# A gMLP and S5 layer on one core: another start for the layer norms, another order of the output pairs with a column split in the last, and a held scaling of C

## The chip, the core and the metric

The kernel runs on one core of one Trainium2 chip. The metric is device microseconds of an execution; the 61 timed runs of the kernel before lie between 261.94 and 264.62 us (standard deviation 0.5). A gMLP is a gated MLP that also mixes rows; S5 is a linear recurrence over the rows. The engines are PE (TensorE, matmul), DVE (VectorE), ACT (ScalarE), POOL (GpSimd) and SP (SyncE, which here issues nearly all DMAs). The profile gives a *span* for each execution: from the core's first recorded instruction to its last. The *time* of the same execution is longer than the span (that difference written "time minus span" below).

## The reference, cut to what matters

```python
xn = layernorm(x)                        # x: 2048 x 640, bf16
# A: a diagonal complex recurrence over 2048 steps, 640 states
Bu = xn @ B_bar.T;  h[t] = Lam_bar * h[t-1] + Bu[t];  yA = 2 * real(h @ C.T) + xn * Dskip
# B: a gated MLP with a mix over rows
z  = gelu(xn @ w_in)                     # 640 -> 1728
z1, z2 = z[:, :864], layernorm(z[:, 864:])
yB = (z1 * (w_sp @ z2 + b_sp[:, None])) @ w_out
out = x + yA + yB
```

## The kernel before

The program is a list of operations with the memory that each reads and writes. A small list scheduler in the kernel's own source, with a guessed duration for each operation, fixes the order of DVE's, ACT's, POOL's and SP's instructions; PE keeps program order. So each change of an operation or a guess can reorder three engines for the whole run.

PE's order is: layer-norm rows transposed tile by tile (128 rows each) and multiplied by the second half of `w_in` (z2, whose results ACT passes through gelu), then `Bu`, then z1, then the row mix by Strassen-Winograd's seven products (the "spatial" stage), then eight output pairs, again by seven products each.

PE writes its results to the banks of a memory called PSUM; an *eviction* is the copy of such a result out of its bank, by ACT or DVE. The *pitch* is the usual distance from one matmul's start to the next.

The layer norm of tile `i`, and the transposition of its rows (cut). Tiles 0 to 5 are transposed by PE and copied from PSUM, tiles 6 to 15 by DMA:

```python
ACT_LN = (5, 8, 11)                  # statistics by two ACT passes; the others by DVE's bn_stats
DMA_T = tuple(range(6, 16))
def ln_x(i):
    if i in ACT_LN:
        act(... ACT.Copy, accum_out=stv[:, i, 0:1] ...)       # sum
        act(... ACT.Square, accum_out=stv[:, i, 1:2] ...)     # sum of squares
        dve(... mean = sum / D ...); dve(... mean * mean ...); dve(... var ...)
    else:
        dve(bn_stats); dve(bn_stats); dve(bn_aggr)
    dve(lambda e: e.tensor_scalar(stv[:, i, 14:15], stv[:, i, 13:14], 1e-5, None, op0=ALU.add), ...)
    pool(lambda e: e.tensor_tensor(rstd, stv[:, i, 14:15], C("half")[:, 0:1], ALU.pow), ...)
    dve(... xn = (x - mean) * rstd ...)
def xn_T(i):
    if i in DMA_T:
        dma("sp", xnTv[:, :, i * 128:(i + 1) * 128], xn.ap(D), ..., transpose=True); return
    pe(five transposes of 128 columns)
    if (i % 2 == 0 or i == 1) and i != 2: act(copy)           # ... else dve(copy)
```

The end of an output pair (cut). `X`, `V`, `W` are PSUM banks, `og` adds the last 96 rows of the sum, `store` is a DMA to the output:

```python
prod("P7", X, False)
# ACT copies X to W (in the last pair to two banks, 192 and 128 columns)
prod("P3", V, False); og(0, 1, V); add(c12); store(0)
prod("P4", X, False); og(1, 0, X); add(c21)
# last pair: store(c21 half, sp); for each part: og(1, 1, part); add(c22 part); store(part)
# other pairs: og(1, 1, W); add(c22); store(1)
```

Of the kernel before, what the change touches and what calls it, by code (L numbers as in the profile page):

```python
# [6 lines left out]
ALU = mybir.AluOpType  # L7
# [21 lines left out]
class _Graph:  # L29
# [57 lines left out]
    def schedule(self):  # L87
# [32 lines left out]
        while left:  # L120
# [23 lines left out]
            if op.nbytes:  # L144
                if op.lat > 2.2:
                    dma_free = max(st + 0.3, dma_free) + op.nbytes / self.DMA_BW_T
                    free[eng] = max(free[eng], dma_free)
                    op.done = max(st + op.occ, dma_free) + 1.7
                else:
                    at = max(st + op.occ + 0.9, dma_free)  # L150
                    dma_free = at + op.nbytes / (self.DMA_BW0 if at < self.DMA_T0 else self.DMA_BW)
                    op.done = dma_free + op.lat - 0.9
            else:
                op.done = st + op.occ + op.lat
# [50 lines left out]
D = 640  # L205
# [9 lines left out]
def bass_parallel_sum__ssm_conv_s5__mixer_gmlp__prompt_kernel(  # L215
# [17 lines left out]
    with _cl.ExitStack() as _stack, nc.Block() as block:  # L233
# [274 lines left out]

        ACT_LN = (5, 8, 11)
        EARLY = (0, 1, 2)  # L510
        HELD = ()
        XNB = 0.0
# [4 lines left out]
        LASTN = 480  # L517
        DMA_T = tuple(range(6, 16))
        xns = {}

        xc_m = z1o_m

        def ln_early(i):

            xm, xc = xs[i], xc_m[i]
            mean, rstd = mrv[:, i, 0:1], mrv[:, i, 1:2]
            mi, ri = mr_m.iv(i * 8, 4), mr_m.iv(i * 8 + 4, 4)
            if i < 2:
                act(lambda e: e.activation(xc.ap(D), xm.ap(D), ACT.Copy, scale=1.0 / D, accum_out=mean),
                    [xm.iv()], [xc.iv(0, 1280), mi], ca(D, acc=1), "lnmean%d" % i)  # L530
            else:
                mean, mi = stv[:, i, 12:13], siv(i, 12, 13)
                early_bn(i)
            dve(lambda e: e.tensor_scalar(xc.ap(D), xm.ap(D), mean, None, op0=ALU.subtract), [xm.iv(), mi], [xc.iv(0, 1280)],
                cd(D, 4) + PTR, "xc%d" % i)

        def early_bn(i):
            x, xm = xs[i].ap(D), xs[i]
            held = [xc_m[2].iv()] if i == 1 else []
            dve(lambda e: e.bn_stats(stv[:, i, 0:6], x[:, 0:320]), [xm.iv()] + held, [siv(i, 0, 6)], 0.41, "bn%da" % i)  # L540
# [4 lines left out]
        def ln_early_std(i):  # L545
            rstd, ri = mrv[:, i, 1:2], mr_m.iv(i * 8 + 4, 4)
            if i < 2:
                early_bn(i)
            dve(lambda e: e.tensor_scalar(stv[:, i, 14:15], stv[:, i, 13:14], 1e-5, None, op0=ALU.add),
                [siv(i, 13, 14)], [siv(i, 14, 15)], 0.07, "lne%d" % i)  # L550
            pool(lambda e: e.tensor_tensor(rstd, stv[:, i, 14:15], C("half")[:, 0:1], ALU.pow),
                 [siv(i, 14, 15), Civ("half")], [ri], 0.5, "rstd%d" % i)

        def ln_early_xn(i):
            xm, xn = xs[i], xn_m[i]
            xns[i] = xn
            mean, mi = (mrv[:, i, 0:1], mr_m.iv(i * 8, 4)) if i < 2 else (stv[:, i, 12:13], siv(i, 12, 13))
            dve(lambda e: e.tensor_scalar(xn.ap(D), xm.ap(D), mean, mrv[:, i, 1:2], op0=ALU.subtract, op1=ALU.mult),
# [4 lines left out]
        def ln_x(i):  # L563
# [4 lines left out]
            if i in ACT_LN:  # L568
                sq = xn_m[i]
                act(lambda e: e.activation(sq.ap(D), x, ACT.Copy, accum_out=stv[:, i, 0:1]),  # L570
                    [xm.iv()], [sq.iv(), siv(i, 0, 1)], ca(D, acc=1), "lnsum%d" % i)
                act(lambda e: e.activation(sq.ap(D), x, ACT.Square, accum_out=stv[:, i, 1:2]),
                    [xm.iv()], [sq.iv(), siv(i, 1, 2)], ca(D, acc=1), "lnsq%d" % i)
                dve(lambda e: e.tensor_scalar(mean, stv[:, i, 0:1], 1.0 / D, None, op0=ALU.mult),
                    [siv(i, 0, 1)], [mi], 0.07, "lnm%d" % i)
                dve(lambda e: e.tensor_tensor(stv[:, i, 2:3], mean, mean, ALU.mult),
                    [mi], [siv(i, 2, 3)], 0.07, "lnmm%d" % i)
                dve(lambda e: e.scalar_tensor_tensor(stv[:, i, 13:14], stv[:, i, 1:2], 1.0 / D, stv[:, i, 2:3],
                                                     op0=ALU.mult, op1=ALU.subtract),
                    [siv(i, 1, 3)], [siv(i, 13, 14)], 0.07, "lnv%d" % i)  # L580
            else:
# [5 lines left out]
                    "bna%d" % i)  # L587
            dve(lambda e: e.tensor_scalar(stv[:, i, 14:15], stv[:, i, 13:14], 1e-5, None, op0=ALU.add),
                [siv(i, 13, 14)], [siv(i, 14, 15)], 0.07, "lne%d" % i)
            pool(lambda e: e.tensor_tensor(rstd, stv[:, i, 14:15], C("half")[:, 0:1], ALU.pow),  # L590
                 [siv(i, 14, 15), Civ("half")], [ri], 0.5, "rstd%d" % i)
            xn = xn_m[i]
# [5 lines left out]
        def xn_T(i, b=None):  # L598
# [15 lines left out]
            if i == 0:  # L614
# [3 lines left out]
                    [xnT_m.iv(k * S * 2, 256) for k in (3, 4)], 0.21, "xnT0b")  # L618
            elif (i % 2 == 0 or i == 1) and i != 2:
                act(lambda e: e.copy(xnTv[:, :, i * 128:(i + 1) * 128], v), [bank(b)], xnT_iv(i, i + 1),  # L620
# [341 lines left out]

        def c_scaled():

            for q in range(5):
                for c, (src, nm) in enumerate(((A_C_re, "r"), (A_C_im, "i"))):
                    dma("sp", cpv[:, c, q, :].rearrange("p (o n) -> p o n", o=1), src[:, q * 128:(q + 1) * 128], [],
                        [cp_m.iv((c * 5 + q) * 1280, 1280)], D * 256, "C%s%d" % (nm, q), transpose=True)
            for q in range(5):
                k1, k2 = C("k")[:, q:q + 1], C("k")[:, 5 + q:6 + q]  # L970
# [3 lines left out]
                act(lambda e, o=ta, im=im, k2=k2: e.activation(o.ap(D), im, ACT.Identity, scale=k2),  # L974
                    [imi, Civ("k")], [ta.iv()], ca(D, ptr=1), "cy%d0" % q)
                act(lambda e, o=tb, re=re, k2=k2: e.activation(o.ap(D), re, ACT.Identity, scale=k2),
                    [rei, Civ("k")], [tb.iv()], ca(D, ptr=1), "cy%d1" % q)

# [55 lines left out]
        def ring(lst, n):  # L1034
            m = lst[n[0] % len(lst)]
            n[0] += 1
            return m

        def spatial(j, banks):
            X, Y, Z = banks  # L1040
# [52 lines left out]
            prod(X, "A22", "T4", False, "P4")  # L1093
            ev(half(c1, 0), X, b1, hiv(c1, 0), "c21_%d" % j)
            zm = z1i[j]
            for h, c in ((0, c0), (1, c1)):
# [85 lines left out]
        def out_pair(j, last=False):  # L1182
# [68 lines left out]
            prod("P7", X, False)  # L1251
            W = bk()
            if last:
                W2 = bk()
                parts = (("act", W, 0, 192), ("sp", W2, 192, HD))
            else:
                parts = (("sp", W, 0, HD),)
            for _, w, c0, c1 in parts:
                act(lambda e, w=w, c0=c0, c1=c1: e.copy(ps[:, w, c0:c1], ps[:, X, c0:c1]), [bank(X)], [bank(w)],  # L1259
                    ca(c1 - c0, psum=True), "u3%d_%d" % (c0, j))  # L1260
            prod("P3", V, False)
            og(0, 1, V)
            add(ov(0, 1), V, fv(t12), "c12b")
            store(0)
            prod("P4", X, False)
            og(1, 0, X)
            add(ov(1, 0), X, bv(1, 0), "c21b")
            def finish():
                for q, w, c0, c1 in parts:
                    og(1, 1, w, c0, c1)  # L1270
                    o = om[1].ap(HD, BF16, 640)
                    dve(lambda e, w=w, c0=c0, c1=c1, o=o: e.tensor_tensor(o[:, c0:c1], ps[:, w, c0:c1], f(t22)[:, c0:c1],
                                                                          ALU.add),
                        [bank(w), t22.iv(c0 * 4, (c1 - c0) * 4)], [om[1].iv(640 + c0 * 2, (c1 - c0) * 2)], cd(c1 - c0),
                        "c22b%d_%d" % (c0, j))
                    if last:
                        store(1, q, HD + c0, HD + c1)
                if not last:
                    store(1)
            if last:  # L1280
                store(1, "sp", 0, HD)
                finish()
            else:
                finish()

        EARLY_AT = (7, 8, 9)
        LATE = 3
        for i in EARLY:
            ln_early(i)
        for i in EARLY:  # L1290
            ln_early_std(i)
# [5 lines left out]
        for i in (3, 4):  # L1297
            ln_x(i)
        z2_mm(0, 0, 2, 2, 5)
# [68 lines left out]
        for gm in g_m:  # L1368
            pool(lambda e, gm=gm: e.memset(gm.ap(32, BF16, 1728), 0.0), [], [gm.iv(1728, 64)], 0.2, "gpad")
        c_scaled()  # L1370
        ct_comb()
        no = [0]
# [21 lines left out]
        for j in range(8):  # L1394
            load_z1(j)
            s_comb(j)
            spatial(j, (0, 1, 2) if j % 2 == 0 else (3, 4, 5))
            if j + 2 < 8:
                for a in ("A21", "A11", "A12", "A22"):
# [83 lines left out]
```

## Time and profile before

| | |
|---|---|
| time, median of the first 3 runs | 263.33 us (262.6 to 263.37) |
| span of the profiled execution (its time: 263.89 us) | 262.1 us |
| PE busy | 255.7 us (98%) |
| DVE busy | 244.6 us |

The waits view of the kernel before, for PE alone. Columns: engine, tile and line, what it waited for, microseconds in total, times, longest.

```profile
PE ps L649 <- DMA arena<-arena: 1.4, 1, 1.4
PE ps L490 <- DVE arena L477: 1.2, 1, 1.2
PE ps L670 <- ACT arena L620: 0.4, 1, 0.4
PE ps L611 <- DVE arena L534: 0.3, 1, 0.3
```

Nothing after 21 us is in this list: PE is dense from there to its last matmul but for three hiccups of 0.65 us together, and the starts of its matmuls lie 183 ns (432 columns) and 136 ns (320 columns) apart. So nearly all that can be shortened lies in the start and the end of the execution, for a change that takes no PE work away.

The timeline of the kernel before: PE around its longest wait, then the end on PE, DVE and ACT's queue. Columns: start, duration of the group, engine, line, operation, out<-in, shapes, count, and in brackets the idle time before it and what ended it.

```profile
13.66 0.44 PE L611 MATMUL ps<-arena 128*128 128x128 bf16 x5
13.94 1.08 PE L670 MATMUL ps<-arena 128*128 128x432 bf16 x5
14.89 0.90 PE L649 MATMUL ps<-arena 128*128 128x432 bf16 x4
...
17.21 2.00 PE L649 MATMUL ps<-arena 128*128 128x432 bf16 x10
20.62 0.72 PE L649 MATMUL ps<-arena 128*128 128x432 bf16 x3 [1.41 <-DMA arena<-arena]
...
258.71 0.44 PE L1213 MATMUL ps<-arena 96*128 96x320 bf16 x3
259.05 0.49 DVE L1227 TENSOR_TENSOR arena<-ps,arena 128x320 bf16<-128x320 f32 x1 [0.73 <-PE ps L1213]
259.46 0.55 DVE L1272 TENSOR_TENSOR arena<-ps,arena 128x192 bf16<-128x192 f32 x2
259.84 0.37 ACTq L373 DMA_DIRECT2D out_dram<-arena  x1
```

L611 are the transposes of a tile (five), L649 and L670 the z2 matmuls. At 20.62 PE has waited for tile 6's transpose by DMA; counted from matmul start to matmul start the stall is 1.58 us over the pitch. At the end three additions on DVE follow the last matmuls one after the other.

### The profile page before, as it was taken

Reading aid. Unit: us, or ns where it says so; the run is one execution under the profiler, and the core shown is the slowest. Engines: PE = TensorE matmul, PEld = TensorE weight load, DVE = VectorE, ACT = ScalarE, POOL = GpSimd, SP = SyncE. Lnnn points to the kernel's source line nnn. Section 1 sums busy time; section 2 is a strip of 40 time slices with the busy share of each in tenths; the row PEclk is TensorE's granted clock in tenths of the full one; section 3 lists DMA queues with packets and bytes.
Section 4 is the critical chain, followed back from the end, with each engine's and each line's share of the span. In section 5 each row is a group of like instructions: output and inputs, shape, how many; then the busy total and the mean of one; then the engine's idle time right before and its main releaser. Section 6 shows DMA issues by size and latency. Waiting matters only on the chain.

```text
span 262.1 us, 4316 instructions
## 1 busy us (share of the span) xinstructions
PE 255.7 (98%) x1488; PEld 151.4 (58%) x1488; DVE 244.6 (93%) x584; ACT 178.8 (68%) x322; POOL 22.6 (9%) x37
## 2 busy tenths in 40 slices
PE   7998999999999999999999999999999999999995
PEld 3544554444446777755555555555556777777773
DVE  5899999698999999999999999899999999999952
ACT  5698999989997445442333385795979996885110
POOL 2445155500000000000000000000000000000000
PEclk9999999999999999999999999999999999999999
DMA  6957859999405763298988968977533455645721
GB/s 196 347 94 123 190 116 238 260 310 188 47 0 117 189 184 135 103 315 141 196 171 180 224 142 200 170 195 188 146 103 105 138 118 133 164 134 151 185 92 54
DMA packets 90276, 42.48 MB, mean 162 GB/s; under 512 B 73006, under 2 KB 90254, under 8 KB 90254
## 3 DMA queue, kind: packets, MB, share of 16 engines
q1 hardware_dynamic: 90110, 42.16, 67.1%
q8 instruction: 12, 0.20, 0.3%
q14 instruction: 10, 0.08, 0.1%
q10 hardware_dynamic: 144, 0.05, 0.1%
HBM read 12.27 MB, written 12.45 MB: 94 GB/s over the span
## 4 chain that ended last, share of the span: by engine, by line
PE 65%; DVE 20%; DMA 8%; issue 4%; ACT 1%; POOL 0%; SPq 0%; DVEq 0%
PE ps L1206 23%; PE ps L649 18%; PE ps L743 16%; DVE arena L1016 5%; PE ps L1059 4%; DMA g_scratch<-arena 4%; DVE arena L794 2%; PE ps L670 2%; DMA arena<-arena 2%; PE ps L1213 2%; DVE arena L1132 1%; DMA arena<-in_B_w_sp_dram 1%; DVE arena L853 1%; DVE arena L1079 1%; DVE arena L772 1%
## 5 line engine op out<-in xcount | busy, mean ns | idle before, releaser
L1059 PE MATMUL ps<-arena 128*128 128x432 bf16 x448 | 82.1, 346 | 0.1
L1059 PEld LDWEIGHTS ps<-arena 128*128 128x128 bf16 x448 | 43.7, 98 | 38.3 <-ACT arena L1072 0.8
L1206 PE MATMUL ps<-arena 128*128 128x320 bf16 x448 | 64.6, 299 | 0.1
L1206 PEld LDWEIGHTS ps<-arena 128*128 128x128 bf16 x448 | 43.4, 98 | 18.1 <-ACT ps L1259 0.5
L649 PE MATMUL ps<-arena 128*128 128x432 bf16 x280 | 51.9, 346 | 1.4 <-DMA arena<-arena 1.4
L849 ACT ACTIVATE arena<-arena 128x512 bf16<-128x512 bf16 x70 | 46.2, 713 | 4.3 <-DVE arena L853 2.9
L649 PEld LDWEIGHTS ps<-arena 128*128 128x128 bf16 x280 | 34.5, 124 | 17.9 <-DMA arena<-arena 1.8
L743 PE MATMUL ps<-arena 128*128 128x512 bf16 x200 | 43.3, 379 | 0.0
L1072 ACT ACTIVATE arena<-ps,arena 128x432 f32<-128x432 f32 (+1 forms) x32 | 19.5, 618 | 22.4 <-PE ps L1059 19.3
L743 PEld LDWEIGHTS ps<-arena 128*128 128x128 bf16 x200 | 19.6, 98 | 23.5
L772 DVE SCALAR_TENSOR_TENSOR arena<-arena 128x512 f32<-128x512 bf16 x35 | 25.5, 742 | 0.1
L748 ACT CAST arena<-ps 128x512 bf16<-128x512 f32 x40 | 22.2, 610 | 3.0 <-PE ps L743 3.0
L1227 DVE TENSOR_TENSOR arena<-ps,arena 128x320 bf16<-128x320 f32 (+1 forms) x40 | 18.7, 483 | 5.8 <-PE ps L1213 4.4
L853 DVE TENSOR_TENSOR arena<-arena 128x1024 bf16<-128x1024 bf16 (+1 forms) x42 | 24.1, 592 | 0.0
L727 ACT ACTIVATE arena<-ps 128x864 bf16<-128x864 f32 x16 | 14.3, 891 | 13.9 <-PE ps L649 12.9
L1016 DVE TENSOR_TENSOR arena<-arena 128x1024 bf16<-128x1024 bf16 x32 | 21.2, 681 | 0.4 <-DMA arena<-in_B_w_sp_dram 0.4
L794 DVE TENSOR_TENSOR arena<-arena 128x512 f32<-128x512 f32 (+2 forms) x40 | 21.2, 547 | 0.0
L777 DVE SCALAR_TENSOR_TENSOR arena<-arena 128x256 bf16<-128x256 bf16 (+1 forms) x35 | 16.6, 476 | 0.0
L774 DVE SCALAR_TENSOR_TENSOR arena<-arena 128x256 bf16<-128x256 bf16 (+1 forms) x35 | 16.4, 474 | 0.0
L1235 ACT COPY ps<-ps 128x320 f32<-128x320 f32 x16 | 6.6, 414 | 13.9 <-PE ps L1206 13.9
L1173 DVE TENSOR_TENSOR arena<-arena 128x640 bf16<-128x640 bf16 x32 | 15.2, 480 | 0.0
L663 ACT ACTIVATE arena<-arena 128x864 bf16<-128x864 bf16 x12 | 11.2, 934 | 0.0
(117 smaller groups left out, 255.7 us busy)
## 6 DMA issues: line engine op xcount, KB each, us to landing
g_scratch<-arena SPq DMA_DIRECT2D x16, 224.0 KB, 2.9
z_scratch<-arena SPq DMA_DIRECT2D x16, 216.0 KB, 2.1
arena<-z_scratch SPq DMA_DIRECT2D x8, 432.0 KB, 4.2
arena<-in_A_x_dram SPq DMA_DIRECT2D x16, 160.0 KB, 3.6
base_scratch<-arena SPq DMA_DIRECT2D x16, 160.0 KB, 2.3
arena<-base_scratch SPq DMA_DIRECT2D x16, 160.0 KB, 2.7
out_dram<-arena SPq DMA_DIRECT2D x15, 160.0 KB, 2.1
arena<-in_B_w_in_dram SPq DMA_DIRECT2D x7, 216.0 KB, 4.0
```

What stands on the lines that cost most here:

```text
L649: r = e.matmul(ps[:, b + h, 0:FG], lhs(k), winv[:, k, hcol * FH + h * FG:hcol * FH + (h + 1) * FG], start=(k == 0), stop=(k == ND - 1))
L743: r = e.matmul(ps[:, b, :], btv[:, ri, k, q * 128:(q + 1) * 128], xnTv[:, k, tq * 512:(tq + 1) * 512], start=(k == 0), stop=(k == ND - 1))
L748: act(lambda e: e.copy(o[:, ri, tq], ps[:, b, :].rearrange("p (m j) -> p j m", j=8)), [bank(b)], [l_m.iv((q * 8 + j) * 1024 + ri * 512 + t ...
L772: dve(lambda e: e.scalar_tensor_tensor(tv, prev, lr, cur, op0=ALU.mult, op1=ALU.add), pr + [l_iv(q, j)] + cr, [t.iv()], cd(512) + PTR, nm ...
L794: tt = lambda o, a, b, op: (lambda e: e.tensor_tensor(o, a, b, op))
L849: act(lambda e, pv=pv, hv=hv, lo=lo, sc=sc: e.activation(pv, hv[:, lo:lo + 2, 1:257], ACT.Identity, scale=sc), [h.iv(), Civ(cn)], [m.iv((q ...
L853: dve(lambda e, mv=mv, lq=lq: e.tensor_tensor(lq, lq, mv, ALU.add), li + [m.iv(0, 1024 * n)], li, cd(512 * n, 2), "fix%s%d%d" % (nm, q0, j))
L1016: dve(lambda e: e.tensor_tensor(o.ap(1024), x.ap(1024), y.ap(1024), op), [x.iv(), y.iv()], [o.iv()], cd(1024, 2), "%s_%d" % (name, j))
L1059: r = e.matmul(ps[:, bk, 0:FG], lv_[:, k, :], rv[k], start=(first and k == 0), stop=(k == 7), skip_group_check=True)
L1072: act(lambda e: e.activation(o, pb(bk), ACT.Identity, bias=bias), [bank(bk)] + bi, [dst], ca(FG, psum=True, ptr=1), name)
L1206: r = e.matmul(ps[:, bk, c0:c1], lf(q), rf(q)[:, c0:c1], start=(first and q == 0), stop=(q == 7), skip_group_check=True)
L1227: dve(lambda e: e.tensor_tensor(o[0][:, c0:c1], ps[:, bk, c0:c1], y[0][:, c0:c1], ALU.add), [bank(bk), y[1]], [o[1]], cd(c1 - c0), "%s_%d" ...
```

## The change

Its intent: take tile 6 off the slow DMA transpose, relieve DVE in the start, let less work follow the last matmul, and keep C's scaling from running ahead of its load (the hold). The scheduler's guess for a DMA transpose is changed too. The diff, cut (marked `...`):

```diff
-                    dma_free = max(st + 0.3, dma_free) + op.nbytes / self.DMA_BW_T
-                    free[eng] = max(free[eng], dma_free)
-                    op.done = max(st + op.occ, dma_free) + 1.7
+                    dma_free = max(st + 1.25, dma_free) + op.nbytes / 270e3
+                    free[eng] = st + 0.65 + op.nbytes / 300e3
+                    op.done = dma_free + 2.2
...
-        ACT_LN = (5, 8, 11)
+        ACT_LN = (3, 6, 10)
+        ACTM = (0, 1)
+        LNE_DVE = (5, 6, 7)
...
-        DMA_T = tuple(range(6, 16))
+        DMA_T = tuple(range(7, 16))
...
-            dve(lambda e: e.tensor_scalar(stv[:, i, 14:15], stv[:, i, 13:14], 1e-5, None, op0=ALU.add),
+            (dve if i in LNE_DVE else pool)(
+                lambda e: e.tensor_scalar(stv[:, i, 14:15], stv[:, i, 13:14], 1e-5, None, op0=ALU.add),
...
-                dve(lambda e: e.tensor_scalar(mean, stv[:, i, 0:1], 1.0 / D, None, op0=ALU.mult), ...
-                dve(lambda e: e.tensor_tensor(stv[:, i, 2:3], mean, mean, ALU.mult), ...
...
-            elif (i % 2 == 0 or i == 1) and i != 2:
+            elif i in (1, 4, 6):
                 act(lambda e: e.copy(xnTv[:, :, i * 128:(i + 1) * 128], v), ...
...
-        c_scaled()
-        ct_comb()
+        c_load()
...
             spatial(j, (0, 1, 2) if j % 2 == 0 else (3, 4, 5))
+            if j == 3:
+                c_scale([u3_of[CY_AT]])        # held until spatial tile 3's u3
+                ct_comb()
...
+            og(1, 1, W)
+            add(ov(1, 1), W, fv(t22), "c22b")
+            if last:
+                store(1, "act", HD, D)
+            for n, (x, c0, c1) in enumerate(parts):     # last pair: 192 and 128 columns, two banks
+                prod("P4", x, False, c0, c1)
+                og(1, 0, x, c0, c1)
+                dve(... c21 columns c0:c1 ...)
+                if last:
+                    store(1, ("sp", "act")[n], c0, c1)
```

More of the change, by code (lines that the diff above doesn't have):

```diff
@@ L517, in bass_parallel_sum__ssm_conv_s5__mixer_gmlp__prompt_kernel @@
         LASTN = 480
-        DMA_T = tuple(range(6, 16))
+        DMA_T = tuple(range(7, 16))
         xns = {}
-        xc_m = z1o_m
+        xc_m = z1o_m + [xn_m[15]]
         def ln_early(i):
@@ L527, in ln_early @@
             mi, ri = mr_m.iv(i * 8, 4), mr_m.iv(i * 8 + 4, 4)
-            if i < 2:
+            if i in ACTM:
                 act(lambda e: e.activation(xc.ap(D), xm.ap(D), ACT.Copy, scale=1.0 / D, accum_out=mean),
@@ L538, in early_bn @@
             x, xm = xs[i].ap(D), xs[i]
-            held = [xc_m[2].iv()] if i == 1 else []
+            held = [xc_m[2].iv()] if i == 1 else xnT_iv(2, 3) if i == 3 else []
             dve(lambda e: e.bn_stats(stv[:, i, 0:6], x[:, 0:320]), [xm.iv()] + held, [siv(i, 0, 6)], 0.41, "bn%da" % i)
@@ L546, in ln_early_std @@
             rstd, ri = mrv[:, i, 1:2], mr_m.iv(i * 8 + 4, 4)
-            if i < 2:
+            if i in ACTM:
                 early_bn(i)
-            dve(lambda e: e.tensor_scalar(stv[:, i, 14:15], stv[:, i, 13:14], 1e-5, None, op0=ALU.add),
-                [siv(i, 13, 14)], [siv(i, 14, 15)], 0.07, "lne%d" % i)
+            (dve if i in LNE_DVE else pool)(
+                lambda e: e.tensor_scalar(stv[:, i, 14:15], stv[:, i, 13:14], 1e-5, None, op0=ALU.add),
+                [siv(i, 13, 14)], [siv(i, 14, 15)], 0.07 if i in LNE_DVE else 0.22, "lne%d" % i)
             pool(lambda e: e.tensor_tensor(rstd, stv[:, i, 14:15], C("half")[:, 0:1], ALU.pow),
-                 [siv(i, 14, 15), Civ("half")], [ri], 0.5, "rstd%d" % i)
+                 [siv(i, 14, 15), Civ("half")], [ri], 0.55, "rstd%d" % i)
         def ln_early_xn(i):
@@ L556, in ln_early_xn @@
             xns[i] = xn
-            mean, mi = (mrv[:, i, 0:1], mr_m.iv(i * 8, 4)) if i < 2 else (stv[:, i, 12:13], siv(i, 12, 13))
+            mean, mi = (mrv[:, i, 0:1], mr_m.iv(i * 8, 4)) if i in ACTM else (stv[:, i, 12:13], siv(i, 12, 13))
             dve(lambda e: e.tensor_scalar(xn.ap(D), xm.ap(D), mean, mrv[:, i, 1:2], op0=ALU.subtract, op1=ALU.mult),
@@ L569, in ln_x @@
                 sq = xn_m[i]
-                act(lambda e: e.activation(sq.ap(D), x, ACT.Copy, accum_out=stv[:, i, 0:1]),
-                    [xm.iv()], [sq.iv(), siv(i, 0, 1)], ca(D, acc=1), "lnsum%d" % i)
-                act(lambda e: e.activation(sq.ap(D), x, ACT.Square, accum_out=stv[:, i, 1:2]),
+                act(lambda e: e.activation(sq.ap(D), x, ACT.Copy, scale=1.0 / D, accum_out=mean),
+                    [xm.iv()], [sq.iv(), mi], ca(D, acc=1), "lnsum%d" % i)
+                act(lambda e: e.activation(sq.ap(D), x, ACT.Square, scale=D ** -0.5, accum_out=stv[:, i, 1:2]),
                     [xm.iv()], [sq.iv(), siv(i, 1, 2)], ca(D, acc=1), "lnsq%d" % i)
-                dve(lambda e: e.tensor_scalar(mean, stv[:, i, 0:1], 1.0 / D, None, op0=ALU.mult),
-                    [siv(i, 0, 1)], [mi], 0.07, "lnm%d" % i)
-                dve(lambda e: e.tensor_tensor(stv[:, i, 2:3], mean, mean, ALU.mult),
-                    [mi], [siv(i, 2, 3)], 0.07, "lnmm%d" % i)
-                dve(lambda e: e.scalar_tensor_tensor(stv[:, i, 13:14], stv[:, i, 1:2], 1.0 / D, stv[:, i, 2:3],
-                                                     op0=ALU.mult, op1=ALU.subtract),
-                    [siv(i, 1, 3)], [siv(i, 13, 14)], 0.07, "lnv%d" % i)
+                dve(lambda e: e.scalar_tensor_tensor(stv[:, i, 13:14], mean, mean, stv[:, i, 1:2],
+                                                     op0=ALU.mult, op1=ALU.subtract, reverse1=True),
+                    [siv(i, 1, 2), mi], [siv(i, 13, 14)], 0.07, "lnv%d" % i)
             else:
@@ L587, in ln_x @@
                     "bna%d" % i)
-            dve(lambda e: e.tensor_scalar(stv[:, i, 14:15], stv[:, i, 13:14], 1e-5, None, op0=ALU.add),
-                [siv(i, 13, 14)], [siv(i, 14, 15)], 0.07, "lne%d" % i)
+            (dve if i in LNE_DVE else pool)(
+                lambda e: e.tensor_scalar(stv[:, i, 14:15], stv[:, i, 13:14], 1e-5, None, op0=ALU.add),
+                [siv(i, 13, 14)], [siv(i, 14, 15)], 0.07 if i in LNE_DVE else 0.22, "lne%d" % i)
             pool(lambda e: e.tensor_tensor(rstd, stv[:, i, 14:15], C("half")[:, 0:1], ALU.pow),
-                 [siv(i, 14, 15), Civ("half")], [ri], 0.5, "rstd%d" % i)
+                 [siv(i, 14, 15), Civ("half")], [ri], 0.55, "rstd%d" % i)
             xn = xn_m[i]
@@ L961, in kappa, with c_load @@
                 R, [Civ("k")], 0.08, "k12")
-        def c_scaled():
+        def c_load():
             for q in range(5):
@@ L968, in c_scaled, with c_scale @@
                         [cp_m.iv((c * 5 + q) * 1280, 1280)], D * 256, "C%s%d" % (nm, q), transpose=True)
+        def c_scale(held):
             for q in range(5):
@@ L974, in c_scaled @@
                 act(lambda e, o=ta, im=im, k2=k2: e.activation(o.ap(D), im, ACT.Identity, scale=k2),
-                    [imi, Civ("k")], [ta.iv()], ca(D, ptr=1), "cy%d0" % q)
+                    [imi, Civ("k")] + held, [ta.iv()], ca(D, ptr=1), "cy%d0" % q)
                 act(lambda e, o=tb, re=re, k2=k2: e.activation(o.ap(D), re, ACT.Identity, scale=k2),
-                    [rei, Civ("k")], [tb.iv()], ca(D, ptr=1), "cy%d1" % q)
+                    [rei, Civ("k")] + held, [tb.iv()], ca(D, ptr=1), "cy%d1" % q)
                 dve(lambda e, re=re, k1=k1, t=ta: e.scalar_tensor_tensor(re, re, k1, t.ap(D), op0=ALU.mult, op1=ALU.add),
@@ L1037, in ring @@
             return m
+        u3_of = {}
         def spatial(j, banks):
@@ L1094, in spatial @@
             ev(half(c1, 0), X, b1, hiv(c1, 0), "c21_%d" % j)
+            u3_of[j] = u3.iv()
             zm = z1i[j]
@@ L1252, in out_pair @@
             W = bk()
+            cp(W, X, "u3")
+            parts = ((X, 0, HD),)
             if last:
-                W2 = bk()
-                parts = (("act", W, 0, 192), ("sp", W2, 192, HD))
-            else:
-                parts = (("sp", W, 0, HD),)
-            for _, w, c0, c1 in parts:
-                act(lambda e, w=w, c0=c0, c1=c1: e.copy(ps[:, w, c0:c1], ps[:, X, c0:c1]), [bank(X)], [bank(w)],
-                    ca(c1 - c0, psum=True), "u3%d_%d" % (c0, j))
+                X2 = bk()
+                parts = ((X, 0, 192), (X2, 192, HD))
+                act(lambda e: e.copy(ps[:, X2, 192:HD], ps[:, X, 192:HD]), [bank(X)], [bank(X2)], ca(HD - 192, psum=True), "u3b")
             prod("P3", V, False)
@@ L1264, in out_pair @@
             store(0)
-            prod("P4", X, False)
-            og(1, 0, X)
-            add(ov(1, 0), X, bv(1, 0), "c21b")
-            def finish():
-                for q, w, c0, c1 in parts:
-                    og(1, 1, w, c0, c1)
-                    o = om[1].ap(HD, BF16, 640)
-                    dve(lambda e, w=w, c0=c0, c1=c1, o=o: e.tensor_tensor(o[:, c0:c1], ps[:, w, c0:c1], f(t22)[:, c0:c1],
-                                                                          ALU.add),
-                        [bank(w), t22.iv(c0 * 4, (c1 - c0) * 4)], [om[1].iv(640 + c0 * 2, (c1 - c0) * 2)], cd(c1 - c0),
-                        "c22b%d_%d" % (c0, j))
-                    if last:
-                        store(1, q, HD + c0, HD + c1)
-                if not last:
-                    store(1)
-            if last:
-                store(1, "sp", 0, HD)
-                finish()
-            else:
-                finish()
+            og(1, 1, W)
+            add(ov(1, 1), W, fv(t22), "c22b")
+            if last:
+                store(1, "act", HD, D)
+            for n, (x, c0, c1) in enumerate(parts):
+                prod("P4", x, False, c0, c1)
+                og(1, 0, x, c0, c1)
+                o, y = om[1].ap(HD), bv(1, 0)
+                dve(lambda e, x=x, c0=c0, c1=c1: e.tensor_tensor(o[:, c0:c1], ps[:, x, c0:c1], y[0][:, c0:c1], ALU.add),
+                    [bank(x), y[1]], [om[1].iv(c0 * 2, (c1 - c0) * 2)], cd(c1 - c0), "c21b%d_%d" % (c0, j))
+                if last:
+                    store(1, ("sp", "act")[n], c0, c1)
+            if not last:
+                store(1)
         EARLY_AT = (7, 8, 9)
         LATE = 3
-        for i in EARLY:
+        CY_AT = 3
+        for i in EARLY[:3]:
             ln_early(i)
-        for i in EARLY:
+        for i in EARLY[:3]:
             ln_early_std(i)
@@ L1297, in bass_parallel_sum__ssm_conv_s5__mixer_gmlp__prompt_kernel @@
         for i in (3, 4):
-            ln_x(i)
+            if i in EARLY:
+                ln_early(i)
+                ln_early_std(i)
+            else:
+                ln_x(i)
         z2_mm(0, 0, 2, 2, 5)
```

## The prediction

> **What bounds it now.** TensorE. Windows view: from 20.6 us (first tile-6 matmul) to 259 us PE is busy all but 0.15 us of every 20. Matmul starts in the trace are 183 ns apart at 432 columns and 136 ns at 320, column count over full clock to within 3 ns. Only four stretches of PE time can be won: the start (first transpose 4.57 us; stalls of 0.53 and 0.58 us until 7.04), the stall before tile 6 (18.86 to 20.62 us, 1.58 us over the pitch, released by a DMA transpose), about 0.7 us in three hiccups at 171, 195 and 200 us, and the tail: the last matmul starts at 258.94, the span ends at 262.08.
>
> **Start.** In before, tile 6 is transposed by DMA: issued at 16.08, landed after 4.5 us (chain of waits). The change transposes it on PE: five 128-column transposes at the trace's 56 ns, +0.28 us, and one ACT copy of 0.69 us. That takes the 1.58 us stall away unless tile 7, now the first by DMA, brings it back. PE then wants tile 7 at about 21.1 us; with the same 4.5 us its normalised rows must be ready by 16.6. In before they are ready at 17.57. DVE sheds, ahead of them: one tile's statistics (about 1.0 us at the pitch of the trace; tiles 3 and 6 go to ACT instead of 5), two of 0.14 us per ACT tile, five "add epsilon" of 0.14 us (to Pool, where the square root is anyway). About 1.7 us, not all on the chain. ACT loses tile 8's two passes (1.85 us) in 14.7 to 17.3. I expect 0 to 0.5 us of stall left. Gain 0.7 to 1.3, say 1.1 us.
>
> **Tail.** In before three DVE adds follow the last matmuls: 492, 347, 282 ns (starts 259.05, 259.46, 259.72), the last store is issued at 260.03 and its landing seen at 261.62. After, c22 is added before the last product, and P4 ends in two column parts, so only a 128-column add (282 ns) follows the last matmul by the same 0.34 us: end near 259.6, store 0.4 us earlier. The eight extra matmuls carry no more columns; the Trainium skill ("TensorE: Matmul & The Clock Gate", Back-to-back issue gap) gives 81 ns sustained at 128 columns with weight loads against 56 isolated; this trace shows 56 for transposes. Cost 0.02 to 0.2 us.  Gain 0.3 us.
>
> **Middle.** Holding C's scaling (ten 0.8 us DVE and ten 0.7 us ACT operations, at 173 to 180 us in before), the reordered DVE, ACT and DMA queues, and 3 us less small DVE work move work that PE doesn't wait for: 0, plus or minus 0.3 us.
>
> **Predicted: 261.9 us, 8 in 10 from 261.1 to 263.0.** Faster by over 2%: 0.01; within 2%: 0.975; slower: 0.015.
>
> **Right if** the PE wait on a DMA transpose near 19 us is gone or under 0.5 us, PE's dense stretch starts about 1 us earlier, and the gap from last matmul to end falls from 3.15 to about 2.8 us. **Wrong if** tile 7's transpose lands late (stall moves, gain near 0), the longer ACT queue delays tile 6's copy, the new order of the queues makes PE wait for a W_sp load, a gate transpose or a scaled C, or 128-column matmuls run at the weight-load rate.

## The result, and the profile after

The changed kernel took 263.09 us (median of 6, 262.81 to 263.32), the kernel before beside it 263.35 us (median of 6). The ratio is 0.9997, with a 95% interval from 0.9979 to 1.0015: the same time. Ratios here are one kernel's runs over the other's of the same rounds, so they aren't quite the ratio of the medians quoted. The predicted 261.9 us was missed by 1.2 us, and the range by 0.1.

And yet the profiled span had fallen from 262.1 to 261.0 us, by 1.1 of the 1.4 us predicted. The waits of PE in the changed kernel:

```profile
PE ps L490 <- DVE arena L477: 1.2, 1, 1.2
PE ps L649 <- ACT arena L620: 0.7, 1, 0.7
PE ps L611 <- DVE arena L536: 0.3, 1, 0.3
PE ps L670 <- DMA arena<-in_B_w_in_dram: 0.2, 1, 0.2
```

The wait for the DMA transpose is gone. A new one has come: L620 is ACT's copy of a transposed tile. The timeline of the changed kernel, same places as shown of before:

```profile
13.61 0.44 PE L611 MATMUL ps<-arena 128*128 128x128 bf16 x5
13.89 1.08 PE L670 MATMUL ps<-arena 128*128 128x432 bf16 x5
15.62 0.91 PE L649 MATMUL ps<-arena 128*128 128x432 bf16 x4 [0.66 <-ACT arena L620]
...
17.74 0.44 PE L611 MATMUL ps<-arena 128*128 128x128 bf16 x5
...
18.23 3.10 PE L649 MATMUL ps<-arena 128*128 128x432 bf16 x16
...
257.73 0.61 PE L1211 MATMUL ps<-arena 128*128 128x128 bf16 x8
258.17 0.22 PE L1218 MATMUL ps<-arena 96*128 96x128 bf16 x1
257.93 0.80 DVE L1276 TENSOR_TENSOR arena<-ps,arena 128x192 bf16<-128x192 f32 x2
257.96 1.13 ACTq L373 DMA_DIRECT2D out_dram<-arena  x2
```

Tile 4's first matmul starts at 15.62 instead of 14.89, though its transposes (L611, five at 13.61) are as early as before. Tile 6 (in the group at 18.23) then runs without a pause. Why the copy is late stands in ACT's timeline of the changed kernel, 10 to 15.6 us (L573 and L575 are the two statistics passes of tile 6, L680 the gelus; here and in the ACT views below the short ACTIVATION_READ_ACCUMULATOR rows are left out):

```profile
10.25 0.61 ACT L680 ACTIVATE arena<-ps,arena 128x432 bf16<-128x432 f32 x1
11.73 0.62 ACT L680 ACTIVATE arena<-ps,arena 128x432 bf16<-128x432 f32 x1 [0.78 <-PE ps L670]
12.34 0.72 ACT L573 ACTIVATE arena<-arena 128x640 bf16<-128x640 bf16 x1
13.06 0.61 ACT L680 ACTIVATE arena<-ps,arena 128x432 bf16<-128x432 f32 x1
13.66 0.73 ACT L575 ACTIVATE arena<-arena 128x640 bf16<-128x640 bf16 x1
14.38 0.52 ACT L680 ACTIVATE arena<-ps 128x432 bf16<-128x432 f32 x1
14.88 0.69 ACT L620 COPY arena<-ps 128x640 bf16<-128x640 bf16 x1
```

The same view of the kernel before, where the passes (L570, L572) are tile 5's:

```profile
11.11 0.73 ACT L570 ACTIVATE arena<-arena 128x640 bf16<-128x640 bf16 x1
11.91 0.62 ACT L680 ACTIVATE arena<-ps,arena 128x432 bf16<-128x432 f32 x1
12.52 0.73 ACT L572 ACTIVATE arena<-arena 128x640 bf16<-128x640 bf16 x1
13.24 0.61 ACT L680 ACTIVATE arena<-ps,arena 128x432 bf16<-128x432 f32 x1
14.14 0.69 ACT L620 COPY arena<-ps 128x640 bf16<-128x640 bf16 x1 [0.20 <-PE ps L611]
```

In before ACT starts a pass at 11.11 and is waiting for PE when the copy comes up. In after ACT stands idle for 0.78 us until 11.73, behind a gelu that PE hasn't fed yet, then works without a gap, and the copy comes last.

The end did what was predicted. In before the last matmul starts at 258.94 us and the span ends at 262.08, a tail of 3.15 us; after it is 258.17 and 260.98, 2.81 us. The Trainium skill ("TensorE: Matmul & The Clock Gate", Back-to-back issue gap) gives 81 ns sustained for matmuls of 128 columns with their weight loads. Here the eight 128-column matmuls of the split product start 55 to 58 ns apart, the 192-column ones 81 to 85, so the page's 81 isn't met at 128 columns here, and the split cost PE nothing that shows. The same skill ("Trainium Kernel Development and Optimization", Key Constraints) says that another issuing queue saves only issue time. No run here tests that alone; nothing contradicts it: the last store on ACT's queue was seen landed 1.74 us after its issue began (1.52 to 2.25 us in the twelve traces with the new tail), the last one of before, on SP, after 1.58 us (1.57 to 1.67 in the six with the old tail).

So the span lost a microsecond and the time didn't. Two theories:

- **A, an unlucky profile.** The one profiled execution of before (263.89 us, longer than the six runs known until then) waited longer than usual, so there was less to win in the start than I read.
- **B, time outside the span.** The change adds something that lies before the first or after the last recorded instruction.

### The profile page after: what moved, and what is told of

Its sections match the earlier page's. It is cut to its first block, busy times and chain, and to the rows that moved or that the text cites. A ratio compares the mean times of both kernels' runs of the same rounds, so it can differ in the third digit from the quotient of the medians.

```text
span 261.0 us, 4323 instructions
## 1 busy us (share of the span) xinstructions
PE 256.0 (98%) x1501; PEld 152.0 (58%) x1501; DVE 243.9 (93%) x565; ACT 179.8 (69%) x323; POOL 26.9 (10%) x50
## 4 chain that ended last, share of the span: by engine, by line
PE 95%; DMA 2%; ACT 1%; SPq 0%; issue 0%; DVE 0%
PE ps L1063 31%; PE ps L1211 23%; PE ps L649 20%; PE ps L743 17%; PE ps L670 2%; PE ps L1218 2%; DMA arena<-in_B_w_in_dram 2%; ACT arena L680 1%; SPq L373 0%; PE ps L611 0%; ACT arena L575 0%; ACT arena L573 0%; ACT arena L620 0%; DVE arena L1276 0%; PE ps L860 0%
## 5 line engine op out<-in xcount | busy, mean ns | idle before, releaser
L1211 PE MATMUL ps<-arena 128*128 128x320 bf16 (+2 forms) x456 | 64.7, 296 | 0.0
L849 ACT ACTIVATE arena<-arena 128x512 bf16<-128x512 bf16 x70 | 46.3, 712 | 8.5 <-DVE arena L853 8.1
L743 PE MATMUL ps<-arena 128*128 128x512 bf16 x200 | 43.3, 379 | 0.0
L743 PEld LDWEIGHTS ps<-arena 128*128 128x128 bf16 x200 | 19.6, 98 | 23.5
L1240 ACT COPY ps<-ps 128x320 f32<-128x320 f32 x24 | 9.9, 413 | 16.5 <-PE ps L1211 16.3
```

Of the source, the lines that this page charges most:

```text
L743: r = e.matmul(ps[:, b, :], btv[:, ri, k, q * 128:(q + 1) * 128], xnTv[:, k, tq * 512:(tq + 1) * 512], start=(k == 0), stop=(k == ND - 1))
L849: act(lambda e, pv=pv, hv=hv, lo=lo, sc=sc: e.activation(pv, hv[:, lo:lo + 2, 1:257], ACT.Identity, scale=sc), [h.iv(), Civ(cn)], [m.iv((q ...
L1211: r = e.matmul(ps[:, bk, c0:c1], lf(q), rf(q)[:, c0:c1], start=(first and q == 0), stop=(q == 7), skip_group_check=True)
```

## The experiments

All were timed against the kernel before on the same chip, in the same rounds. "Start", "tail", "hold" and "DMA model" name the parts of the diff. The number of instructions of each engine is that of the built program: before has PE 3023, DVE 677, ACT 378, SP 222, POOL 55; after has PE 3040, DVE 658, ACT 378, SP 219, POOL 67. Spans are listed for every run to 0.1 us, so means of spans and of differences are good to that. Each batch ran on another chip, and the mean span of before differs between the batches, from 261.28 to 261.74 us; so a difference of spans from different batches is less sure than its standard error says. (after's second six runs were with e1 to e4; no spans of before were kept beside its first six.)

| run | time, median | mean span | mean of time minus span | ratio to before (95%) |
|---|---|---|---|---|
| before, 61 runs of five batches | | 261.43 | 1.87 (48 of 61 under 1.9) | |
| after, 12 runs (first result and e2) | | 261.11 | 2.18 (2.12 to 2.22) | |
| e1 before again | 263.10 | 261.25 | 1.90 | 1.0001 (0.9978 to 1.0025) |
| e2 after again | 263.59 | 261.32 | 2.18 | 1.0015 (0.9990 to 1.0039) |
| e3 tail only | 263.37 | 260.85 | 2.39 (1.79 to 3.03) | 1.0004 (0.9979 to 1.0028) |
| e4 start only | 264.76 | 262.48 | 2.31 (2.16 to 2.91) | 1.0064 (1.0031 to 1.0097) |
| e5 after, SP + 4 | 263.84 | 261.89 | 2.16 | 1.0025 (1.0005 to 1.0045) |
| e6 after, copy first | 263.16 | 260.98 | 2.18 | 0.9996 (0.9970 to 1.0022) |
| e7 after without hold | 263.18 | 261.55 | 2.16 | 1.0017 (0.9982 to 1.0052) |
| e8 after, both edits | 264.03 | 261.70 | 2.18 | 1.0024 (1.0004 to 1.0043) |
| e9 before, POOL + 12 | 263.40 | 261.25 | 2.15 (2.12 to 2.16) | 1.0010 (0.9988 to 1.0032) |
| e10 after, epsilon on DVE | 263.69 | 261.83 | 2.00 (1.76 to 2.53) | 1.0023 (1.0003 to 1.0044) |
| e11 after, tile 5 on ACT | 264.02 | 261.85 | 2.33 (2.13 to 2.69) | 1.0037 (1.0017 to 1.0056) |
| e12 tail, PE + 4 | 262.69 | 261.10 | 1.81 (1.77 to 1.85) | 0.9976 (0.9949 to 1.0002) |
| e13 before, POOL + 4 | 263.37 | 261.52 | 1.83 | 0.9992 (0.9964 to 1.0021) |
| e14 before, POOL + 28 | 263.01 | 261.15 | 1.84 | 0.9978 (0.9947 to 1.0010) |
| e15 after, POOL + 16 | 262.90 | 261.22 | 1.81 (1.77 to 1.85) | 0.9990 (0.9967 to 1.0013) |
| e16 tail, PE + 4, again | 263.14 | 261.25 | 1.79 (1.77 to 1.84) | 0.9990 (0.9970 to 1.0009) |

The ratios alone settle little: their intervals are about 0.5 us wide on each side. What settles things is time minus span, which repeats to 0.03 us in most kernels, and the stalls in the traces.

### e1 and e2: both kernels again

No edit.

> The kernel before, unchanged, to see every run's span beside its time. Theory A (the profile of before fell on an execution with a long wait for tile 6): the spans of its fast runs average about 261.1 us, a microsecond under the profiled 262.1, and time minus span is about 2.2 us as in the runs of after. Theory B (the span did shrink by 1.1 us but time outside the span grew): spans stay near 261.5 to 262.1 and time minus span is about 1.8 us. Ratio to before 1.000 within 0.15%.

> The changed kernel, unchanged, in five more rounds beside before on one chip. Both theories: 0.998 to 1.000 of before (0 to 0.5 us gained); theory A wants a smaller run-to-run spread than before, as the first tile by DMA has slack; a profile again with a wait of 0.6 to 0.9 us for the ACT copy of tile 4 before PE at about 15 us and none for a DMA transpose.

Both theories had a part of it. The span of before averages 261.43 us over 61 runs (standard error 0.06), so the profiled 262.1 was an execution 0.7 us longer than the mean (A). And time minus span is about 1.8 us in most runs of before but 2.12 to 2.22 in all twelve of after (B). Put together over all batches: span -0.31 us, outside +0.31 us, time 0.00. The second number is safe; the first isn't: in the one batch that has both kernels' spans, before averages 261.27 us (17 runs) and after 261.32 (6 runs). The smaller spread that A wanted hardly showed (0.44 us standard deviation of the span against 0.50).

Eight traces have the start of before (its own, e1, e3, e9, e12, e13, e14, e16): PE's stall at tile 6 is 1.19 to 1.58 us there, 1.36 in the mean, and the one I planned with was the longest. Five have after's unedited start (after, e2, e4, e7, e15): a stall of 0.66 to 0.89 us before tile 4, 0.83 in the mean, plus the 0.28 us of tile 6's transposes. The start is worth 1.36 - 0.83 - 0.28 = 0.25 us at most. Counted whole, from the third z2 matmul to the end of z2, PE needs 31.62 us in the mean of the eight and 31.45 in the mean of the five: 0.17 us.

### e3 and e4: one part alone

e3 is before with the new order and split of the output pairs; e4 is before with the layer-norm and transpose part, without DMA model, hold or tail. The edits are those hunks of the diff.

> Before with only the new order of the output pairs and the split of the last product. If the tail gain is real and lies inside the measured time: 0.3 us less than before (ratio 0.9988), gap from last matmul start to span end 2.8 instead of 3.15 us. Theory B (the end of the program on ACT's queue costs outside the span): no gain in time though the span falls by 0.3.

> Before with only the layer-norm and transpose part (statistics of tiles 3, 6, 10 on ACT, epsilon on Pool, tile 6 transposed by PE), without the new DMA model, C hold or tail. Theory A: within 0.2 us of before in time, as a wait of 0.6 to 0.9 us on ACT before tile 4 plus 0.28 us of transposes take the place of a stall that is typically 1 us. My prediction's theory: 1.1 us less (ratio 0.996).

e3: the tail was 2.58 us, the span 0.58 under before's mean, but the time stayed, because time minus span scattered from 1.79 to 3.03. In the profiled execution (2.74), the trace's DMA records show a 16 KB fetch of instructions at 262.42 us, 1.75 us after the last instruction of the span.

e4: neither theory had this. It was 1.7 us slower. The waits view of e4 for PE:

```profile
PE ps L1059 <- ACT arena L1072: 0.7, 2, 0.5
PE ps L649 <- ACT arena L620: 0.7, 1, 0.7
```

The second is the wait for tile 4's copy again. The first is new: spatial matmuls waited for ACT's evictions at 150 and 178 us. At 150 the scheduler had now placed two scalings of C ahead of the eviction (L974 and L976, from 148.62 to 150.08). At 178 it was another ACT operation (L849), which had waited 1.38 us for DVE. (PE lost 0.43 and 0.63 us there, from start to start.)

### e5: four more SP instructions

In before's trace the last 8 KB instruction block is fetched 0.68 us before the span ends, in after's 0.16 us after it, and SP's stream is three instructions shorter. My first explanation for the 0.3 us was that fetch.

```diff
+        pad_s = _stack.enter_context(nc.semaphore("s_pad"))
                 r.then_inc(sems[op.cnt[0]], 16 if op.nbytes else 1)
+                if op.name == 'z1st0':
+                    for _ in range(4):
+                        e.sem_inc(pad_s)
```

> The changed kernel with four extra instructions on SP (each adds one to a semaphore that nobody reads), so that SP has 223 instructions (after 219, before 222). Fetch theory: the last fetch of an 8 KB instruction block moves from 0.16 us after the end of the span to about 0.7 us or more before it, and time minus span falls from 2.17 to 1.8 us in every run, with the same span: 0.4 us less time than after. Rival (the 0.4 us outside the span comes from the two stores on ACT's queue or from Pool's extra work): time minus span stays at 2.17.

The fetch did move, to 2.26 us before the end of the span, and time minus span stayed at 2.16 us (2.13 to 2.19). The theory fell: SP's last fetch isn't what costs. (e15, below, agrees from the other side: its trace has that fetch 0.15 us after the end, and time minus span is 1.81.) The rival is left.

### e6: the copy ahead of a gelu

```diff
-        z2_mm(3, 0, 2, 0, 5)
+        z2_mm(3, 0, 2, 0, 5, later=True)
         xn_T(4, 0)
+        z2_half(3, 0, 2, after=xnT_iv(4, 5))    # this gelu reads what the copy writes
```

> The changed kernel, with ACT's copy of transposed tile 4 put ahead of the gelu of tile 3's first half: only ACT's order differs. If the new 0.83 us stall before tile 4 is ACT's queue: the copy starts at about 14.4 instead of 14.88, the stall falls to 0.3 to 0.4 us, PE's later work starts 0.4 to 0.5 us earlier and span and time fall by as much. If the stall isn't worth anything (a later wait takes it back): span as after, about 261.1.

A miss in its main number. The copy did run before that gelu, but started at 14.61, and the stall was 0.97 us, no shorter:

```profile
13.29 0.73 ACT L575 ACTIVATE arena<-arena 128x640 bf16<-128x640 bf16 x1
14.01 0.61 ACT L680 ACTIVATE arena<-ps,arena 128x432 bf16<-128x432 f32 x1
14.61 0.69 ACT L620 COPY arena<-ps 128x640 bf16<-128x640 bf16 x1
```

Another gelu took its place ahead of the copy (the timeline of e6 on ACT). One gelu's position wasn't the cause; the two passes of tile 6 in front of everything were not yet tried.

### e7: without the hold

e7 is after without the hunks that hold C's scaling.

> The changed kernel without the hold of C's scaling (DMA model, start and tail kept; instruction counts of SP and PE as after). If the hold is what keeps ACT's evictions on time once the start is changed: stalls of PE on the spatial evictions near 150 and 178 us come back as in the start-only run, 0.5 to 1.2 us more than after. If the DMA model alone does that: within 0.2 us of after.

The profiled execution shows no stall at 150 or 178 us, and the median is 263.18. The stated reading for that case is that the changed DMA model, not the hold, keeps the evictions on time; but e7 differs from e4 by the new tail too, so the DMA model alone isn't shown to do it. One run of the six took 266.04 us at a granted clock of 0.993; I don't explain it. The hold itself showed no worth.

### e8: both edits

e6's and e5's edits together.

> Copy first and four SP instructions together. If both causes are right and add: time 0.8 to 0.9 us under after and 0.6 to 1.0 us under before (ratio 0.996 to 0.998), time minus span 1.8 us. If either is wrong, about half of that.

Neither gain came, as both reasons had been wrong; it was even slower than before by 0.24%. Only the four SP instructions set it apart from e6, and its mean span is 261.70 us against 260.98. e5, with the same four, was long too (261.89). Why is open.

### e9: twelve more POOL instructions in the kernel before

In the change thirteen of the sixteen additions of epsilon moved to POOL, and its stream grew by twelve instructions. Here the kernel before gets twelve instructions that do nothing (the edit of e5 with `op.name == 'z2r8'` and 12).

> The kernel before with twelve extra instructions on Pool (each adds one to a semaphore that nobody reads, after the second of the z2 norms, when Pool has nothing else to do): Pool has 67 instructions as in after (before 55), all else is before's. Pool theory (the time after the last instruction grows with Pool's instruction stream): time minus span is 2.17 us in every run instead of 1.8, the span as before (261.3): 0.35 us slower. Rival (it comes from DVE's shorter stream or the stores): 1.8 as before.

All four runs had 2.12 to 2.16 us, the eleven of before beside them 1.82 in the mean, and the spans were alike (261.25 and 261.37). Twelve idle instructions on an engine that is 9% busy cost 0.32 us outside the span. This is theory B's cause, shown by itself; whether the time lies before the first recorded instruction or after the last, the traces don't tell.

### e10: epsilon back on DVE

```diff
-        LNE_DVE = (5, 6, 7)
+        LNE_DVE = tuple(range(16))
```

> The changed kernel with all additions of epsilon back on DVE, so Pool has 55 instructions. Pool theory: time minus span falls to 1.8 us. Span: my prediction's theory (DVE's small operations lie on the chain of the start) would make it up to 0.7 us longer than after; the ACT-queue theory (DVE isn't what PE waits for at the start) leaves it within 0.2 us.

POOL has 55 instructions again, and four of six runs have 1.76 to 1.84. The other two (2.19 and 2.53) are like e3's scatter; the profiled one of these two has a 16 KB instruction fetch 1.55 us after the span's end. The stall before tile 4 was 0.79 us, so DVE's additions weren't on the chain there. The span was 0.7 us longer than after's, but not from the start: the waits view of e10 shows spatial matmuls waiting for another ACT copy, again by the new order.

```profile
PE ps L1063 <- ACT ps L1085: 0.8, 2, 0.6
PE ps L649 <- ACT arena L620: 0.6, 1, 0.6
```

### e11: tile 5 instead of tile 6 on ACT

```diff
-        ACT_LN = (3, 6, 10)
+        ACT_LN = (3, 5, 10)
```

> The changed kernel with tile 5's statistics on ACT instead of tile 6's (as in before). Tile 5's x lands about 0.7 us before tile 6's, so ACT can do the first pass while it now idles (10.85 to 11.73 us in after) and the copy of tile 4 comes after fewer gelus. ACT-queue theory: the stall before tile 4 falls from 0.83 to under 0.3 us, the tile-6 stall doesn't come back, and span falls by 0.5 us or more, to about 260.6. If the tile-6 rows from DVE come late instead, PE waits for them near 17 us and the span stays.

The timeline of e11 on PE:

```profile
13.86 0.44 PE L611 MATMUL ps<-arena 128*128 128x128 bf16 x5
14.14 1.08 PE L670 MATMUL ps<-arena 128*128 128x432 bf16 x5
15.09 0.91 PE L649 MATMUL ps<-arena 128*128 128x432 bf16 x4
...
17.20 0.44 PE L611 MATMUL ps<-arena 128*128 128x128 bf16 x5
...
17.69 3.56 PE L649 MATMUL ps<-arena 128*128 128x432 bf16 x17
```

ACT's timeline of e11 at tile 5's two passes and the copy, other lines left out:

```profile
11.16 0.74 ACT L573 ACTIVATE arena<-arena 128x640 bf16<-128x640 bf16 x1
12.72 0.73 ACT L575 ACTIVATE arena<-arena 128x640 bf16<-128x640 bf16 x1
14.34 0.69 ACT L620 COPY arena<-ps 128x640 bf16<-128x640 bf16 x1 [0.20 <-PE ps L611]
```

The first pass now fills the time in which ACT stood idle, and ACT waits for PE at the copy, as in before. The stall before tile 4 is gone, and tile 6 starts at 17.69 instead of 18.23, with 0.28 us lost later at tile 7. So the ACT queue of the start, filled by tile 6's late statistics, is what took the gain back. In e11's trace PE needs 30.8 us from its third z2 matmul to the end of z2, in the traces of after's start 31.5 us, in those of before's 31.5 to 31.8. But the span didn't fall (261.85 us in the mean; before beside it 261.37). The same new order lost 0.17 to 0.22 us at each of four spatial tiles (154 to 168 us), and time minus span scattered like e3's.

### e12 and e16: the tail, with four more PE instructions

Kernels with 3036 (e3) or 3038 (e10, e11) PE instructions scattered in time minus span; 3040 (after) didn't. The traces of those three show a 16 KB fetch 1.55 to 1.80 us after the end of the span.

```diff
 # on e3's kernel, with e5's edit at another operation, so on PE:
+                if op.name == 'T0':
+                    for _ in range(4):
+                        e.sem_inc(pad_s)
```

> The tail-only kernel with four extra instructions on PE (after the first transposes, where PE waits anyway), so PE has 3040 instructions as in after (tail-only 3036), Pool 55 as in before. In the tail-only trace a 16 KB instruction block was fetched 1.75 us after the end of the span and time minus span scattered from 1.8 to 3.0. PE-stream theory: here that fetch moves before the end, time minus span is 1.8 in nearly every run, span 0.3 to 0.4 under before: 0.3 us less time (ratio 0.9988), faster than before and after. Rival (the second store on ACT's queue scatters the end): time minus span scatters as in tail-only.

> The tail with four PE instructions once more, because its first ratio (0.9976, interval to 1.0002) was better than its parts explain. The parts (tail 0.3 to 0.4 us, nothing outside the span) say 0.9985; the first measurement says 0.9976. Time minus span 1.8.

All twelve runs had 1.77 to 1.85 us. In e12's trace PE's last 16 KB block is fetched at 257.47, before the end. The second store on ACT's queue is still there, so the rival falls. The tail's gain now seems to reach the time: ratios of 0.9976 and 0.9990, that is 0.6 and 0.3 us, neither clear of 1 by its own interval. The first is too good: e14, in the same batch, has 0.9978 with none of the change. The parts (mean span 261.18 against 261.43, outside 1.80 against 1.87) come to 0.3 us.

### e13 and e14: how POOL's length costs

e9's edit with 4 and with 28 instructions.

> Before with four extra Pool instructions (59; before 55, the twelve-more kernel 67). If the time after the span grows with each Pool instruction (0.34 us for twelve): time minus span 1.93 us. If it is a step somewhere between: 1.82 or 2.15.

> Before with twenty-eight extra Pool instructions (83). Growth with each instruction: time minus span 2.6 us. A step passed once: 2.15, as with twelve more.

59 instructions: 1.83 us. 83: 1.84. Only 67 cost. Neither growth nor one step fits; what is left is the place at which POOL's stream ends. Which places cost, and through what, no run here tells. One trace of each kernel gives a hint: with 83 instructions (e14, e15) the queue that carries the 8 KB instruction blocks has one fetch more, at 53.2 and 50.9 us, well before the end; the traces with 55, 59 and 67 don't have it.

### e15: the change with 83 POOL instructions

e5's edit with `op.name == 'z2r8'` and 16.

> The changed kernel with sixteen more Pool instructions (83, a length that cost nothing in before; after has 67, the length that cost 0.33 us). If the cost outside the span hangs on where Pool's stream ends, not on how long it is: time minus span is 1.8 us in nearly every run (after: 2.17), span as after (about 261.1), time 0.35 us under after and 0.3 to 0.5 under before (ratio 0.998 to 0.999). If something else of the change (DVE's or SP's shorter stream, the order of the stores) also holds it: 2.15.

Six runs of six had 1.77 to 1.85 us (after: 2.12 to 2.22). So the place of POOL's end holds the whole of the missing 0.3 us, and the shorter streams of DVE and SP and the order of the stores hold none. The time was 263.03 us in the mean, against 263.32 for before beside it. The ratio, 0.9990 (0.9967 to 1.0013), isn't clear of 1.

## Why the prediction was wrong, point by point

- **What bounds it: right.** No stall outside the start and the tail was worth much in either kernel. In the trace of before z2's end and the start of the output pairs lie 154.40 us apart, in those of after and e2 154.31 and 154.25.
- **The start: the step that failed** (1.1 us predicted, 0.17 to 0.25 us found). "I expect 0 to 0.5 us of stall left. Gain 0.7 to 1.3, say 1.1 us." Tile 7 did land in time, as argued. But the stall came back at tile 4, where I hadn't looked: ACT had been given tile 6's two passes, and tile 4's copy waited behind them (0.83 us in the mean). I had named a late copy by ACT as what could make the prediction wrong, for tile 6, and put no time on it. I counted the 1.85 us that ACT loses after 14.7 us and not that its queue had no gap from 11.73 on. e11 shows the cause: with tile 5's passes there the stall before tile 4 is 0.
- **The start, its size: mis-sized.** I took 1.58 us of stall from one execution. Eight traces give 1.36 us. What was left to win is 0.25 us at most.
- **The tail: right.** Predicted 0.3 us; six traces with the old tail have 3.13 to 3.23 us from the last matmul's start to the end, twelve with the new one 2.57 to 3.30, 2.82 in the mean: 0.34 us less. It isn't even: the three traces of the tail alone (e3, e12, e16) have 2.58 us, the three of after's own program (after, e2, e15) 2.81 to 2.99, with the last store seen landed 0.2 to 0.4 us later. Why is open.
- **The middle: right in size for after itself** ("0, plus or minus 0.3 us"), wrong as a rule: e4, e10 and e11 lost 0.7 to 1.5 us there against after's trace, by reordering. I also had C's scaling at the wrong place: before runs it from 152 to 178 us, after from 149 to 177, and e7, without the hold, from 148; so the hold held back next to nothing.
- **From span to time: the assumption that I didn't state.** I took every microsecond of span for one of time. POOL's twelve more instructions cost 0.31 to 0.37 us outside the span (after against before, 0.31; e9 against before beside it, 0.32; after against e15, 0.37), as much as the tail gives. e9 shows it alone, e15 takes it away.

The sum, in means over all batches: span 261.43 to 261.11 us, outside 1.87 to 2.18, time the same. I cannot split the span's 0.3 us finely into start and tail, nor be sure of it: the standard error is 0.13 us on after's mean, and the batches differ by more.

Left open: why 67 POOL instructions cost and 55, 59 and 83 don't; why 13 of 61 runs of before also had over 1.9 us outside; why e5 and e8 had longer spans than after (e5's profiled execution lost 1.5 us to a late x tile at the start, but its six other runs were long as well); and whether a start like e11's, with an order of the spatial stage that costs nothing, would be worth its 0.65 us. Before with the new tail and four idle PE instructions is about 0.3 us under both by its parts; two batches put it there, neither beyond doubt. By their ratios e15 (0.9990) and e14 (0.9978, four runs) can't be told from it.

## What to carry to other kernels

When work moves to an engine "that isn't the bottleneck", look at that engine's queue in the very microseconds in question: if it has no gap there, whatever follows in its order is late, also for tiles that the change doesn't touch. Before you count on a wait seen in one profile, look at whether that execution was a typical one; its time against the median of the others says so at once. And when a span falls and the time doesn't, compare time minus span for every run: here the place where an idle engine's instructions end was worth as much as the reordered tail.

## What the Trainium skill lacked or had wrong

- "Runtime: NRT & Kernel Launch", Instruction fetch mechanics, calls the cost of crossing an instruction block "mostly hidden". Here the place where a stream ends cost time outside the span: 0.32 us for POOL with 67 instructions (0 with 59 or 83), and up to 1.2 us for PE with 3036 (1.79 to 3.03 us outside the span, in one execution with a block fetched 1.75 us after its end), against 1.77 to 1.85 with 3040. The page says nothing of a cost at the end of a stream; that a fetch is the reason is likely for PE and not shown for POOL.
- The same section names blocks of 16 KiB. With the settings of these runs that holds for one instruction queue (fetches of 16,384 bytes, one for every 257 PE instructions in the mean of after's trace, so PE's); on the other the fetches are of 8,192 bytes.
- "TensorE: Matmul & The Clock Gate", Back-to-back issue gap, has 81 ns sustained for 128 columns with weight loads. The split product's eight ran at 55 to 58 ns, each with its own weight load. The same sentence has about 131 ns for 512 columns; here 200 of them in a row, each with its own weight load (L743), start 216 ns apart.
